# Attention output reloaded in two transfers a unit, with added waits between transfers

## The chip, the cores and the metric

The kernel runs on one core of a Trainium2 chip. The metric is the device time of one launch in microseconds (us); the kernel before takes 477.96 us, the median of three runs. On one core, TensorE (PE in the profile) multiplies, VectorE (DVE), ScalarE (ACT) and GpSimd (POOL) do the elementwise work, and SyncE (SP) issues the transfers, which the core's 16 DMA engines carry out.

## The reference

The input x has 2048 rows of 512 numbers. One layer normalization feeds two branches, whose product is added back to x.

```python
xn = layernorm(x)
q, k, v = split(xn @ wqkv)               # 32 heads of 16
# window of 8 positions, 2 apart: idx = pos - [0, 2, ..., 14], masked below 0
a = softmax(einsum(q, k[idx]) / 4)       # 8 logits for each row and head
s = einsum(a, v[idx]) @ wo               # attention, output projection 512 x 512
h = xn @ w1 + b1                         # 512 -> 1792
g = silu(relu(h) ** 2 @ w2 + b2)         # 1792 -> 512
out = x + s * g
```

## The kernel before

**Precision.** All large matmuls work on operands that are split into a high and a low part; a product takes three passes (high by high, high by low, low by high). So one block f of the down projection takes twelve matmuls with outputs of 128x512 (four row tiles by three passes), and the output projection of one row tile twelve as well (four parts of D by three passes). The splits cost ACT one instruction (the high part) and DVE or POOL one (the rest).

**First stage** (until about 267 us). The normalized rows are multiplied with wqkv. The results go to DRAM (`sq`, `sk`, `sv`) and come back unit by unit, a unit u being 256 rows (eight in all), in a layout that spreads eight groups of 64 columns (four heads) times 16 blocks of 16 rows over the 128 partitions. There DVE works the attention: products of k and q (`pr`), sums to logits (`L`), exponentials on ACT (`Lp`), products with v (`pv`), sums. The attention's output of a unit is written to DRAM, `so[g, row, 64]`. Beside it TensorE computes the up projection for the first and the second half of F; its outputs `u` stay on the chip for the rows of the chunks 0 and 1 and go to DRAM (`su`) for chunks 2 and 3, from where they come back as `ut`. DVE still works on the attention of the later units through most of the second stage.

**Second stage** (from about 267 us). A chunk c is 512 rows (four in all, each with two units, four row tiles t and four accumulators `pb`). For each block f of 128 of the 14 in F, `make_h` (line 1273) squares u on ACT and forms the rest on DVE or POOL, which gives the two parts of `h`; `down` adds twelve matmuls `pb<-w,h`. In a name such as h0_6 the first number is the chunk and the second the first block of the pair of tiles in it (h0_6 holds blocks 6 and 7). Chunk 0 also brings in w2 (`w2r` raw, one 128x512 transfer for each f, then split into `w`) and the output projection's weights: `load_wo` (line 1371) fetches each of `rwo0` and `rwo1` with two transfers of 256 KB, whose source is an access pattern of [4 groups of 128 rows, 32 rows, 512 columns], and `split_wo` (line 1377) makes `wot` of them. After the last block of a chunk comes the output projection of its first two row tiles (24 matmuls `pw<-wot,oT`), then the next chunk's blocks, and inside these the other two tiles.

**The attention's way back.** `load_o(u)` (line 1320) reads a unit of `so` into `oq`, of which there is one buffer; `trans_o(t)` (line 1329) transposes the half of it that belongs to row tile t in 32x32 blocks on DVE (`oTf`) and takes the high part on ACT (`oT`); `lowo` (line 1338) takes the rest; `out_product` (line 1341) multiplies with `wot`. In a tile's name the number is u for `oq`, and t for `oTf` and `oT`.

**What sets the order.** The program is built twice. In the first, the draft, every instruction is recorded with a price (`Book.add`, line 153), a list scheduler runs over them with these prices (a transfer: 600 ns to issue, then its bytes at 250 bytes a nanosecond on one wire shared by all), and the best of six rounds gives for every engine the order of its instructions, and for each "E" instruction whether it goes to DVE or POOL (`arrange`, line 377). The second program has the same instructions and a dependency between neighbours on each engine that keeps that order without a semaphore. Data and buffers bring their own waits. All transfers but those that load code are issued from SP in the order of the draft; eight semaphores serve them in turn, so that each transfer also waits for the one eight places ahead of it. Because everything passes through the recorder, every line of the profile reads L159, and tiles tell the instructions apart.

Of the kernel before, what the change touches and what calls it, by code (L numbers as in the profile page):

```python
# [11 lines left out]
F32 = mybir.dt.float32  # L12
FR = mybir.dt.float32r
AF = mybir.ActivationFunctionType
# [3 lines left out]
P = 128  # L18
S = 2048
# [11 lines left out]
UP = 256  # L31
NU = S // UP

GR = 8
CH = D // GR
# [43 lines left out]
def elements(ap):  # L79
    n = 1  # L80
    for d in ap.shape[1:]:
        n *= d
    return n


class Book:
# [66 lines left out]
    def add(self, key, name, f, a, k):  # L153
        n = len(self.ops)
        engine = key
        if key == "E":
            engine = self.plan[1][n] if self.plan else "V"
            f = getattr(f[engine], name)
        ins = f(*a, **k)  # L159
        out = k["out"] if "out" in k else a[0]  # L160
        outs = [out] + ([k["accum_out"]] if "accum_out" in k else [])
        ins_ = [*(a if "out" in k else a[1:]), *(x for i, x in k.items() if i not in ("out", "accum_out"))]
        ins_ = [x for x in ins_ if isinstance(x, bass.AP)]
        two = sum(x.space != bass.MemoryType.PSUM and elements(x) > 1 for x in ins_) > (name != "tensor_scalar")
        if key == "E":
            op = Op(n, "E", ins, {e: self.price(e, name, k, ins_, out) for e in "VG"}, True)
        elif name == "dma_start":
            moved = 4
            for d in out.shape:
                moved *= d  # L170
            op = Op(n, "S", ins, 600, moved=moved)
        else:
            op = Op(n, engine, ins, self.price(engine, name, k, ins_, out),
                    engine == "V" and two or engine == "G" and elements(out) > 1 and name != "memset")
        if self.first:
            if op.engine in self.heads:
                self.heads[op.engine].starts.append(op)
                op.waits += 1
            self.heads[op.engine] = op
        func = next((x for x in a if isinstance(x, mybir.ActivationFunctionType)), None)  # L180
        op.table = func if func in (AF.Exp, AF.Silu) else None
        op.stream = self.in_stream
        self.ops.append(op)
        if engine == "P":
            if "P" in self.last:
                self.edge(self.last["P"], op)
            self.last["P"] = op
        for x, writes in [(x, False) for x in ins_] + [(x, True) for x in outs]:
            r = self.region(x)
            if r is None:  # L190
                continue
            t, p0, p1, m = r
            writes = writes or t.space == "PSUM"
            if t not in op.tiles:
                op.tiles.append(t)
                if not t.users:
                    used = self.firsts.setdefault(t.slot, [])
                    if len(used) >= t.bufs:
                        t.behind = used[-1]
                    used.append(op)  # L200
                if t.behind not in (None, op):
                    t.behind.starts.append(op)
                    op.waits += 1
                t.users.append(op)
            kept = []
            for other, w, q0, q1, k_ in t.log:
                if (w or writes) and other is not op and p0 < q1 and q0 < p1 and m & k_:
                    self.edge(other, op)
                if not (writes and p0 <= q0 and q1 <= p1 and k_ & ~m == 0):
                    kept.append((other, w, q0, q1, k_))  # L210
            kept.append((op, writes, p0, p1, m))
            t.log = kept
        return ins
# [138 lines left out]
    def tails(self, order=None):  # L352
# [21 lines left out]
        top = max(tail)  # L374
        return [top - t for t in tail]

    def arrange(self):
        if self.plan is None:
            order, best = None, None
            for _ in range(ROUNDS):  # L380
                end, order = self.forward(self.tails(order))
                if best is None or end < best[0]:
                    best = end, [op.n for op in order], [op.given for op in self.ops]
            return best[1:]
        order = [self.ops[n] for n in self.plan[0]]
        for op in self.ops:
            op.given = self.plan[1][op.n]
        for e in "PVAGS":
            line = [op for op in order if op.given == e]
            for a, b in zip(line, line[1:]):  # L390
                self.tc.add_manual_dep(b.ins.ins, a.ins.ins.name, mybir.DependencyInfo(
                    mybir.DependencyClass.NoSync, mybir.DependencyReason.DATA), reason="order")


class Kept:
# [47 lines left out]
def trace(ctx: ExitStack, tc: tile.TileContext, plan, x, wqkv, wo, w1, b1, w2, b2, out):  # L443
# [4 lines left out]
    PE, V, A, G, E = (Recorded(book, n, e) for n, e in zip(  # L448
        "PVAGE", (nc.tensor, nc.vector, nc.scalar, nc.gpsimd, dict(V=nc.vector, G=nc.gpsimd))))
    dma = Recorded(book, "S", nc.sync).dma_start  # L450

    def pool(name, stack=ctx, after=(), **k):
        return Pool(book, stack.enter_context(tc.tile_pool(name=name, bufs=1, **k)), name, after)
# [125 lines left out]
    so = dram.tile([GR, S, CH], F32, name="so")  # L579
# [157 lines left out]
    mv, means, rs, shifts, xn, xb, pTs, seen, odd = ({} for _ in range(9))  # L737
# [291 lines left out]
    for a in range(2, NT, 2):  # L1029
        n, t = {2: 2, 4: 1}.get(a, 0), a + 2  # L1030
# [273 lines left out]
    p2 = pool("p2", ctx, (px, pstg, p2a, tpool))  # L1304
# [13 lines left out]
    oqs, oTs = {}, {}  # L1318

    def load_o(u):  # L1320

        if u in oqs:
            return
        oqs[u] = p2.tile([P, UP // 64, 2, 2, CH], F32, name=f"oq{u}", tag="oq")
        for g in range(GR):
            src = so[g, u * UP:(u + 1) * UP, :].rearrange("(b p e) c -> p b (e c)", p=32, e=2)
            dma(oqs[u][32 * (g // 2):32 * (g // 2) + 32, :, g % 2].rearrange("p b e c -> p b (e c)"), src)

    def trans_o(t):
        src = p2.tile([P, 512], F32, name=f"oTf{t}", tag="rwo", bufs=2)  # L1330
        src = src.rearrange("p (g n) -> p g n", g=4)
        V.transpose(out=src.rearrange("p (g h) (b n) -> p b g h n", h=2, n=32),
                    in_=oqs[t // 2][:, :, :, t % 2].rearrange("p b g (h c) -> p b g h c", c=32))
        oTs[t] = p2.tile([P, 2, 4, P], FR, name=f"oT{t}", tag="oT", bufs=3)
        A.activation(oTs[t][:, 0], src, AF.Copy)
        seen[t] = src

    def lowo(t):
        E.tensor_sub(oTs[t][:, 1], seen.pop(t), oTs[t][:, 0].bitcast(F32))

    def out_product(t, ps, cols=slice(0, D)):
        o = oTs[t]
# [50 lines left out]
    for c in range(NCH):  # L1393
        last = c == NCH - 1
        t0 = c * TPC
        for f in range(NF):
# [7 lines left out]
            if c:  # L1404
                if f < 2:
                    finish(t0 - 4 + f, E)
                if f == 2:
                    load_o(c * 2 - 1)
                    load_r(t0 - 2)
                    load_r(t0 - 1)  # L1410
                elif f == 4:
                    trans_o(t0 - 2)
                    trans_o(t0 - 1)
                elif f == 5:
                    lowo(t0 - 2)
                    lowo(t0 - 1)
                elif f == 6:
                    out_product(t0 - 2, psT(f"pw{t0 - 2}"))
                elif f == 7:
                    finish(t0 - 2, E)  # L1420
                    out_product(t0 - 1, psT(f"pw{t0 - 1}"))
                elif f == 8:
                    finish(t0 - 1, E)
            if f >= 7:
                load_o(c * 2)
            if f in (9, 10) and not last:
                load_r(t0 + f - 9)
            if f == 11:
                for i in range(2):
                    trans_o(t0 + i)  # L1430
            if f == 12:
                for i in range(2):
                    lowo(t0 + i)
                load_o(c * 2 + 1)
# [18 lines left out]
        else:  # L1453
# [15 lines left out]
            for j in range(2, TPC):  # L1469
                n = D // 2 if j == TPC - 1 else D  # L1470
# [28 lines left out]
```

## Time and profile before

| | |
|---|---|
| Runs, us | 479.42, 475.67, 477.96; median 477.96 |
| Profiled execution, us | 475.35, of which the span 473.6 |
| Mean granted TensorE clock | 0.996 |
| PE busy | 463.6 us, 98% of the span |
| DVE, ACT, POOL busy | 85%, 62%, 59% |
| Transfers of `oq` | 64 of 64 KB, eight a unit |
| Share of the chain that ended last | PE 89%, DMA 6%, all else 1% or less each |

The profile shows one execution. Its groups give, for each kind of instruction, the engine, the operation, output and inputs by tile names and the count, then busy time, the mean duration and the idle time just before with what ended it. In rows of a timeline stand the start in us, the duration of all instructions in the row, the engine and the group, the count behind an "x", and in brackets the idle time ahead of it and what it waited for. Rows of a stretch of time give its bounds and length, the busy time of PE, PEld (weight load), DVE, ACT and POOL with the number of instructions, then the granted TensorE clock, the busy share of the 16 DMA engines and what they moved in GB/s. Rows of the chain of waits give the start, the length and what ran or was waited for. DMA rows on SP (SPq) show how long issuing took, waits included.

### The profile page before, as it was taken

What the parts mean: (1) busy time and instruction counts of PE and PEld (TensorE: products, weight loads), DVE (VectorE), ACT (ScalarE), POOL (GpSimd) and SP (SyncE); (2) the same over time, 40 slices, a digit from 0 to 9 for tenths busy, and PEclk for the clock granted to TensorE, in tenths of its full rate; (3) what the DMA queues carried; (4) which work ended last, traced back from release to release, by engine and by line L of the source; (5) the groups of instructions that cost most, each with busy time, mean ns of one, the idle gap of its engine ahead of it and who ended that gap; (6) DMA issues with size and microseconds to landing.
All of it is one profiled execution on the core that took longest, in us unless ns stands there. A gap on an engine that the chain in (4) does not pass through costs nothing.

```text
span 473.6 us, 6218 instructions
## 1 busy us (share of the span) xinstructions
PE 463.6 (98%) x2037; PEld 380.6 (80%) x2037; DVE 403.9 (85%) x341; ACT 291.7 (62%) x567; POOL 280.5 (59%) x297
## 2 busy tenths in 40 slices
PE   8999999999999999999999997999999999999996
PEld 6788888888788888888888785788888888888886
DVE  4987977999999998999999984899999999992213
ACT  5756968866564558468584965795249535844311
POOL 2286324336997699956453567876674566376330
PEclk9999999999999999999999998999999999999999
DMA  8799899999689977641860558748894994443102
GB/s 276 210 219 280 287 220 285 253 230 252 184 226 275 261 239 201 227 105 47 209 155 2 156 144 205 193 124 251 174 255 115 259 238 142 146 144 91 45 19 72
DMA packets 77901, 87.78 MB, mean 185 GB/s; under 512 B 6956, under 2 KB 59436, under 8 KB 77868
## 3 DMA queue, kind: packets, MB, share of 16 engines
q1 hardware_dynamic: 77868, 87.38, 69.4%
q8 instruction: 16, 0.26, 0.2%
q14 instruction: 17, 0.14, 0.1%
HBM read 53.75 MB, written 30.47 MB: 178 GB/s over the span
## 4 chain that ended last, share of the span: by engine, by line
PE 89%; DMA 6%; POOL 1%; ACT 1%; DVE 1%; issue 1%; SPq 0%; POOLq 0%
PE pb L159 25%; PE uX L159 16%; PE pq L159 13%; PE pm L159 12%; PE pw L159 9%; PE uZ L159 8%; DMA w2r<-in_B_w 5%; PE uY L159 4%; DMA oq<-so 2%; PE warm L159 1%; SPq L159 0%; PE pxT L159 0%; POOL h L159 0%; DVE wq L159 0%; POOL w L159 0%
## 5 line engine op out<-in xcount | busy, mean ns | idle before, releaser
L159 PE MATMUL pb<-w,h 128*128 128x512 f32 x592 | 152.1, 394 | 3.6 <-POOL h L159 3.5
L159 PEld LDWEIGHTS pb<-w,h 128*128 128x128 f32 x592 | 111.6, 190 | 29.7 <-POOL h L159 5.8
L159 DVE TENSOR_TENSOR pr<-k,qp 128x2048 f32<-128x2048 f32 x32 | 72.8, 2276 | 7.3 <-ACT qp L159 5.6
L159 DVE TENSOR_REDUCE v<-pv 128x256 f32<-128x2048 f32 x32 | 73.0, 2281 | 0.7
L159 DVE TENSOR_TENSOR pv<-v,Lp 128x2048 f32<-128x2048 f32 x32 | 72.8, 2276 | 0.6
L159 DVE TENSOR_REDUCE L<-pr 128x128 f32<-128x2048 f32 x32 | 72.7, 2273 | 0.5
L159 POOL TENSOR_TENSOR h<-ut,h 128x512 fp32r<-128x512 f32 x26 | 33.3, 1295 | 34.6 <-ACT ut L159 33.3
L159 POOL TENSOR_TENSOR h<-u,h 128x512 fp32r<-128x512 f32 (+1 forms) x32 | 33.0, 1050 | 24.1 <-ACT u L159 16.8
L159 PE MATMUL pw<-wot,oT 128*128 128x512 f32 (+1 forms) x204 | 45.5, 376 | 0.0
L159 PEld LDWEIGHTS pw<-wot,oT 128*128 128x128 f32 x204 | 36.8, 188 | 7.1
L159 DVE TENSOR_TENSOR z<-z,pw 128x512 f32<-128x512 f32 (+1 forms) x17 | 11.0, 650 | 26.2 <-ACT z L159 14.4
L159 ACT ACTIVATE ut<-ut 128x512 f32<-128x512 f32 x42 | 24.8, 624 | 12.1 <-DMA ut<-su 12.0
L159 PE MATMUL pq<-wq,XA 128*128 128x512 f32 x122 | 31.5, 391 | 0.3 <-DVE wq L159 0.3
L159 ACT ACTIVATE u<-uX,b1t 128x512 f32<-128x512 f32 x28 | 19.2, 687 | 18.2 <-PE uX L159 14.6
L159 ACT ACTIVATE h<-ut 128x512 fp32r<-128x512 f32 x28 | 16.4, 625 | 22.3 <-PE pb L159 10.5
L159 POOL TENSOR_TENSOR u<-u,more 128x512 f32<-128x512 f32 x14 | 18.2, 1297 | 17.4 <-ACT more L159 16.7
L159 POOL TENSOR_TENSOR oT<-oTf,oT 128x512 fp32r<-128x512 f32 x16 | 20.7, 1295 | 11.3 <-ACT oT L159 11.3
L159 PEld LDWEIGHTS pq<-wq,XA 128*128 128x128 f32 x122 | 22.7, 188 | 5.4 <-DVE wq L159 0.7
L159 ACT ACTIVATE stg<-pm 128x512 f32<-128x512 f32 x30 | 18.0, 599 | 14.3 <-PE pm L159 12.0
L159 ACT ACTIVATE u<-u 128x512 f32<-128x512 f32 (+1 forms) x54 | 26.4, 528 | 0.2
L159 ACT ACTIVATE stg<-pq 128x512 f32<-128x512 f32 x24 | 14.3, 598 | 13.4 <-PE pq L159 10.8
L159 ACT ACTIVATE h<-u 128x512 fp32r<-128x512 f32 (+1 forms) x36 | 17.4, 528 | 5.9 <-PE pb L159 5.8
(166 smaller groups left out, 990.4 us busy)
## 6 DMA issues: line engine op xcount, KB each, us to landing
k<-sk SPq DMA_DIRECT2D x8, 960.0 KB
v<-sv SPq DMA_DIRECT2D x8, 960.0 KB, 7.1
su<-u SPq DMA_DIRECT2D x28, 256.0 KB, 2.5
ut<-su SPq DMA_DIRECT2D x28, 256.0 KB, 4.5
x<-in_A_x SPq DMA_DIRECT2D x16, 256.0 KB, 4.9
sk<-stg SPq DMA_DIRECT2D x8, 512.0 KB, 3.3
sq<-stg SPq DMA_DIRECT2D x8, 512.0 KB, 5.0
sv<-stg SPq DMA_DIRECT2D x8, 512.0 KB, 6.0
```

Of the source, the lines that this page charges most:

```text
L159: ins = f(*a, **k)
```

## The change

There are three edits. `load_o` fetches a unit with two transfers of 256 KB in place of eight of 64 KB: each fills all 128 partitions with 2 KB, read from four groups (outermost, 2·S·64 elements apart), 32 runs in each and 512 contiguous numbers a run. A partition then holds eight neighbouring rows of a group where it held rows 64 apart two by two; so the transposed rows stand in another order, and `trans_o` and `lowo` write `oT` through `positions`, with neighbouring elements four apart. And `landed` adds waits: for each transfer past the program's first part it looks up in the draft schedule which earlier transfer is the last one that has ended when this one starts, and makes it wait for that one, where that is later than what earlier transfers have waited for already.

```diff
--- before.py
+++ after.py
@@ -172,6 +172,7 @@
         else:
             op = Op(n, engine, ins, self.price(engine, name, k, ins_, out),
                     engine == "V" and two or engine == "G" and elements(out) > 1 and name != "memset")
+        op.early = self.first
         if self.first:
             if op.engine in self.heads:
                 self.heads[op.engine].starts.append(op)
@@ -374,13 +375,23 @@
         top = max(tail)
         return [top - t for t in tail]
 
+    def landed(self, order):
+
+        out, line, last = [], [op for op in order if op.moved], -1
+        for i, op in enumerate(line):
+            done = max((j for j in range(i) if line[j].end <= op.start), default=-1)
+            if done > last and not op.early:
+                out.append((op.n, line[done].n))
+                last = done
+        return out
+
     def arrange(self):
         if self.plan is None:
             order, best = None, None
             for _ in range(ROUNDS):
                 end, order = self.forward(self.tails(order))
                 if best is None or end < best[0]:
-                    best = end, [op.n for op in order], [op.given for op in self.ops]
+                    best = end, [op.n for op in order], [op.given for op in self.ops], self.landed(order)
             return best[1:]
         order = [self.ops[n] for n in self.plan[0]]
         for op in self.ops:
@@ -390,6 +401,9 @@
             for a, b in zip(line, line[1:]):
                 self.tc.add_manual_dep(b.ins.ins, a.ins.ins.name, mybir.DependencyInfo(
                     mybir.DependencyClass.NoSync, mybir.DependencyReason.DATA), reason="order")
+        for n, m in self.plan[2]:
+            self.tc.add_manual_dep(self.ops[n].ins.ins, self.ops[m].ins.ins.name, mybir.DependencyInfo(
+                mybir.DependencyClass.Sync, mybir.DependencyReason.DATA), reason="landed")
 
 
 class Kept:
@@ -1321,22 +1335,26 @@
 
         if u in oqs:
             return
-        oqs[u] = p2.tile([P, UP // 64, 2, 2, CH], F32, name=f"oq{u}", tag="oq")
-        for g in range(GR):
-            src = so[g, u * UP:(u + 1) * UP, :].rearrange("(b p e) c -> p b (e c)", p=32, e=2)
-            dma(oqs[u][32 * (g // 2):32 * (g // 2) + 32, :, g % 2].rearrange("p b e c -> p b (e c)"), src)
+        oqs[u] = p2.tile([P, 2, UP // 64, 2, CH], F32, name=f"oq{u}", tag="oq")
+        run = UP // 32 * CH
+        for g in range(2):
+            row = so[g, u * UP:u * UP + 1, :]
+            src = bass.AP(tensor=row.tensor, offset=row.offset, ap=[[2 * S * CH, GR // 2], [run, 32], [1, run]])
+            dma(oqs[u][:, g].rearrange("p b e c -> p (b e c)"), src)
 
     def trans_o(t):
         src = p2.tile([P, 512], F32, name=f"oTf{t}", tag="rwo", bufs=2)
-        src = src.rearrange("p (g n) -> p g n", g=4)
-        V.transpose(out=src.rearrange("p (g h) (b n) -> p b g h n", h=2, n=32),
-                    in_=oqs[t // 2][:, :, :, t % 2].rearrange("p b g (h c) -> p b g h c", c=32))
+        V.transpose(out=src.rearrange("p (g h b n) -> p b g h n", g=2, h=2, n=32),
+                    in_=oqs[t // 2][:, :, :, t % 2].rearrange("p g b (h c) -> p b g h c", c=32))
         oTs[t] = p2.tile([P, 2, 4, P], FR, name=f"oT{t}", tag="oT", bufs=3)
-        A.activation(oTs[t][:, 0], src, AF.Copy)
-        seen[t] = src
+        seen[t] = src.rearrange("p (g b n) -> p g b n", g=4, n=32)
+        A.activation(positions(t, 0), seen[t], AF.Copy)
+
+    def positions(t, a):
+        return oTs[t][:, a].rearrange("p g (n b) -> p g b n", b=4)
 
     def lowo(t):
-        E.tensor_sub(oTs[t][:, 1], seen.pop(t), oTs[t][:, 0].bitcast(F32))
+        E.tensor_sub(positions(t, 1), seen.pop(t), positions(t, 0).bitcast(F32))
 
     def out_product(t, ps, cols=slice(0, D)):
         o = oTs[t]
```

The transfers that SP issues fall from 312 to 264. The order of the instructions changes from about 268 us on. Three places show it. In the rows, the number behind an underscore only tells tiles of one name apart.

First the transfers on SP at the beginning of the second stage. Before:

```order
L159 DMA w2r8_2819<-in_B_w2 128x512
L159 DMA rwo0_2816<-in_A_wo 128x1x512 x2
L159 DMA oq0_2939<-so_155 32x4x128 x8
L159 DMA rwo1_2841<-in_A_wo 128x1x512 x2
L159 DMA w2r9_2844<-in_B_w2 128x512
L159 DMA w2r10_2864<-in_B_w2 128x512
L159 DMA v4_1539<-sv_154 128x1x1920
L159 DMA w2r11_2885<-in_B_w2 128x512
```

Now:

```order
L159 DMA w2r8_2819<-in_B_w2 128x512
L159 DMA rwo0_2816<-in_A_wo 128x1x512 x2
L159 DMA oq0_2939<-so_155 128x1x512 x2
L159 DMA rwo1_2841<-in_A_wo 128x1x512 x2
L159 DMA v4_1539<-sv_154 128x1x1920
L159 DMA w2r9_2844<-in_B_w2 128x512
L159 DMA w2r10_2864<-in_B_w2 128x512
L159 DMA w2r11_2885<-in_B_w2 128x512
```

The eight transfers of oq0 are two, of the shape that `rwo0` and `rwo1` have, and v4 (960 KB) has moved ahead of w2r9 and w2r10. Of the added waits, rwo1's second transfer waits for rwo0's first, v4 for rwo0's second, and w2r9 for rwo1's second. Some ten transfers later, the two of oq1 stand between ut2_0 and ut2_1, where the eight stood behind ut2_2.

Then ACT in the same stretch. Here `wot<-rwo1` is the split of the output projection's weights, h0_6 the squares of blocks 6 and 7 of chunk 0, qp5_2 a copy of q for the attention. Before:

```order
L159 ACTIVATE wot_2750<-rwo0_2816 128x512 x2
L159 ACTIVATE qp5_2_1553<-q5_1520 128x512
L159 ACTIVATE u06_2607<-u06_2607 128x2x256
L159 ACTIVATE wot_2750<-rwo1_2841 128x512
L159 ACTIVATE h0_6_2869<-u03_2454 128x512 x2
L159 ACTIVATE u03_2454<-u03_2454 128x2x256 x2
L159 ACTIVATE w28_2821<-w2r9_2844 128x512
L159 ACTIVATE w210_2866<-w2r10_2864 128x512
L159 ACTIVATE wot_2750<-rwo1_2841 128x512
```

Now:

```order
L159 ACTIVATE wot_2750<-rwo0_2816 128x512 x2
L159 ACTIVATE wot_2750<-rwo1_2841 128x512 x2
L159 ACTIVATE qp5_2_1553<-q5_1520 128x512
L159 ACTIVATE h0_6_2869<-u03_2454 128x512 x2
L159 ACTIVATE u03_2454<-u03_2454 128x2x256 x2
L159 ACTIVATE u06_2607<-u06_2607 128x2x256
L159 ACTIVATE w28_2821<-w2r9_2844 128x512
L159 ACTIVATE w210_2866<-w2r10_2864 128x512
L159 ACTIVATE h0_8_2915<-u04_2589 128x512 x2
```

Both copies of rwo1 stand ahead of qp5_2 and h0_6 now, where one of them stood behind qp5_2 and the other behind h0_6 and w210.

Last ACT in chunk 1, where TensorE works on its blocks 0 to 4; ut2_3 and the like are rectified there as they come back for chunk 2. Before:

```order
L159 ACTIVATE oT2_3215<-oTf2_3213 128x512
L159 ACTIVATE oT3_3219<-oTf3_3217 128x512
L159 ACTIVATE ut2_3_3394<-ut2_3_3394 128x512
L159 ACT_TABLE_LOAD
L159 ACTIVATE Lp5_1586<-L5_1543 128x512
L159 ACTIVATE ut2_5_3429<-ut2_5_3429 128x512
L159 ACTIVATE oT4_3388<-oTf4_3386 128x512
L159 ACTIVATE h1_4_3181<-u02_2445 128x512 x2
```

Now:

```order
L159 ACTIVATE oT2_3203<-oTf2_3201 128x4x4x32
L159 ACTIVATE oT3_3207<-oTf3_3205 128x4x4x32
L159 ACTIVATE ut2_3_3376<-ut2_3_3376 128x512
L159 ACT_TABLE_LOAD
L159 ACTIVATE Lp5_1586<-L5_1543 128x512
L159 ACTIVATE ut2_5_3405<-ut2_5_3405 128x512
L159 ACTIVATE ut2_7_3501<-ut2_7_3501 128x512
L159 ACTIVATE ut2_9_3541<-ut2_9_3541 128x512
L159 ACTIVATE h1_4_3169<-u02_2445 128x512 x2
```

The squares of blocks 4 and 5 (h1_4) follow ut2_7 and ut2_9 now, of which both stood behind them, and oT4 has gone behind them.

## The prediction

> **What bounds the kernel now.** I read the page first (span, busy times, shares of the chain), then busy times by stretch, then TensorE's timeline where a stretch loses time, then the chain of waits and the other engines' timelines there. The profiled execution took 475.35 us, its span is 473.6; the median of the runs is 477.96, and the mean of all four executions 477.1. Less than 1% either way, some 4.8 us, can't be told from no change here.
>
> ```profile
> span 473.6 us, 6218 instructions
> PE 463.6 (98%) x2037; PEld 380.6 (80%) x2037; DVE 403.9 (85%) x341; ACT 291.7 (62%) x567; POOL 280.5 (59%) x297
> PE 89%; DMA 6%; POOL 1%; ACT 1%; DVE 1%; issue 1%; SPq 0%; POOLq 0%
> ...
> 133.50:266.65 133.15, 133.15 (x589) 110.24 (x588) 130.36 (x80) 88.28 (x167) 94.69 (x106) 1.00 0.63 176
> 266.65:311.87 45.22, 41.62 (x170) 32.04 (x168) 34.68 (x22) 31.90 (x66) 32.12 (x28) 0.96 0.67 172
> 311.87:464.35 152.48, 152.48 (x674) 126.29 (x673) 121.71 (x86) 79.94 (x146) 85.45 (x70) 1.00 0.58 156
> ...
> 312.03 5.44 PE pw L159 x24
> ```
>
> TensorE is the bound: it has no idle time at all from 133.5 to 266.65 us and from 311.87 to 464.35 us. Only the stretch between, which is chunk 0, loses time. Its 14 blocks of 12 matmuls, at 5.44 / 24 = 0.227 us each by the last row, are 38.1 us of work in 45.2 us: 7.1 us are lost. That is the most that the change can win, 1.5%.
>
> ```profile
> 283.65 1.01 PE L159 MATMUL pb<-w,h 128*128 128x512 f32 x3
> 286.37 7.36 PE L159 MATMUL pb<-w,h 128*128 128x512 f32 x24 [1.71 <-POOL h L159]
> 295.02 2.33 PE L159 MATMUL pb<-w,h 128*128 128x512 f32 x9 [1.29 <-POOL h L159]
> ...
> PE pb L159 <- POOL h L159: 3.5, 4, 1.7
> ...
> 287.00:289.00 2.00, 2.00 (x7) 1.51 (x6) 0.00 (x0) 0.00 (x0) 0.56 (x1) 0.51 1.05 234
> ```
>
> Of the 7.1 us, 3.5 are waits for `h`, the longest ahead of block 6 at 286.37 us. The clock granted behind that pause is 0.51, and the 24 matmuls take 7.36 us where they would take 5.44: 1.9 more. The rest is slow first matmuls beside the pauses.
>
> Why was `h` late? ACT makes its high part, and ACT stood still:
>
> ```profile
> 275.97 1.14 ACT L159 ACTIVATE wot<-rwo 128x512 fp32r<-128x512 f32 x2
> 277.01 0.58 ACT L159 ACTIVATE qp<-q 128x512 f32<-128x512 f32 x1
> 282.73 0.63 ACT L159 ACTIVATE wot<-rwo 128x512 fp32r<-128x512 f32 x1 [4.57 <-DMA rwo<-in_A_wo]
> 283.26 1.14 ACT L159 ACTIVATE h<-u 128x512 fp32r<-128x512 f32 x2
> ...
> 268.14 8.07 DMA oq<-so
> 277.48 11.73 DMA w2r<-in_B_w
> ...
> 276.24 1.13 SPq L159 DMA_DIRECT2D rwo<-in_A_wo  x2
> ```
>
> It waited 4.57 us for the first half of rwo1, and the squares of blocks 6 and 7 stood behind that wait. The chain says the same in transfers: oq0's first, issued at 268.14, landed 8.07 us later at 276.2, then rwo1's two went out, and w2r9, issued at 277.48, landed at 289.2 behind them.
>
> **What the new transfers cost.** No transfer of oq of the new form is in the trace, but `rwo0` has the same one: 256 KB to all partitions, with four groups as the outermost part of the source. After its issue a stretch shows it nearly alone:
>
> ```profile
> 268.50:270.00 1.50, 1.50 (x8) 1.18 (x7) 1.50 (x2) 1.50 (x6) 0.20 (x1) 1.00 0.28 97
> 273.00:274.00 1.00, 1.00 (x6) 0.84 (x5) 1.00 (x1) 1.00 (x3) 1.00 (x3) 1.00 0.27 99
> 283.00:287.00 4.00, 2.29 (x10) 1.38 (x9) 3.85 (x2) 2.44 (x5) 1.95 (x2) 1.00 1.04 188
> ```
>
> The 16 DMA engines are busy for a share of 0.28 (4.4 of 16) at 97 GB/s, while a mixed load reaches 1.04 and 188 GB/s, or 234 by the row of 287 above. At 97 GB/s, 262 KB take 2.70 us; the two for a unit take 5.4 us. I take this value. The lower bound is the rate of all engines, 1.14 us each at 230 GB/s.
>
> [...]
>
> **Chunk 0, step by step.** T is the time at which rwo1's second half lands. At 276.2 the two halves of rwo0 are through (ACT splits them at 275.97 without a wait). oq0's first transfer, though only 64 KB and with a share for every engine, landed no sooner, so an engine works in the order of issue. I take it that two transfers of one form use the same engines; then oq0's two and rwo1's two stand in one line of four times 2.70 us: 276.2 + 10.8 = 287.0. v4 (960 KB), now right behind them, moves beside them. Before, rwo1's second half, which had v4 and three w2r beside it, landed between 282.7 and 289.2, so up to 6.5 us for 2.7 us of work. I add 1.5 us for v4: T = 288.5, with 287.0 as the end without contention.
>
> ACT now splits both halves of rwo1 ahead of qp5_2 and h0_6, so it stands still until T, where before it went on at 282.7 with the first half. Block 6 then follows by T + 0.6 (split) + 0.5 (qp5_2) + 3.1 (from h's start at 283.26 to TensorE's at 286.37) = 292.7, against 286.4: **+6.3**. The pause grows from 1.7 to 8 us, so the half clock lasts somewhat longer: I take 2.5 us for its 1.9, **+0.6**. The later stall of 1.29 us and one of 0.29 are covered then: **−1.6**. The end of chunk 0 moves by **+5.3** us, from 311.9 to 317.2.
>
> [...]
>
> w2r9 waits for rwo1's second half too, so the queue (w2r9 to w2r11, q6, xr, w2r12, w2r13) starts at 288.5; block 9 is needed only at 292.7 + 3 x 2.72 = 300.9, and I cost that at nothing. If v4 or w2r came 5 us later, block 9 would be late by some 2 us.
>
> **Chunk 1.** qp5_2 also starts DVE's next attention step:
>
> ```profile
> L159 DVE TENSOR_TENSOR pr<-k,qp 128x2048 f32<-128x2048 f32 x32 | 72.8, 2276 | 7.3 <-ACT qp L159 5.6
> L159 DVE STREAM_TRANSPOSE oTf<-oq x16: 669/700/711, 295.4 to 438.6; 128x512 f32<-128x512 f32 x16
> L159 DVE TENSOR_TENSOR w212r<-w2r,w x1: 1106/1106/1106, 303.1 to 303.1; 128x512 fp32r<-128x512 f32 x1
> ...
> 306.15 0.71 ACT L159 ACTIVATE h<-u 128x256 fp32r<-128x256 f32 x2
> 314.02 0.73 ACT L159 ACTIVATE h<-u 128x256 fp32r<-128x256 f32 x2
> 318.16 1.28 ACT L159 ACT_TABLE_LOAD   x1
> ...
> ut<-su SPq DMA_DIRECT2D x28, 256.0 KB, 4.5
> ```
>
> In the new order DVE does five attention steps of 2.28 us, three parts of `h` of 1.1 us (as w212r) and two transposes of 0.70 before oq0's second transpose is over: 16.1 us. From T + 1.1 and half a microsecond of hand-overs that is 306.4, where oq's single buffer is free. oq1's two transfers (5.4 us) then go ahead of ut2_1 (4.5 us from issue to landing): 316.3. ACT rectifies ut2_1 ahead of h1_0, and from the start of h1_0 to the end of h1_1 it took 7.9 us (306.15 to 314.02): 324.4, and the low part 0.7 more, 325.1. TensorE wants block 1 at 317.2 + 5.44 + 2.72 = 325.4: just in time, 0. Then ACT does h1_2 (2.5 us), two oT (1.0), ut2_3 (0.6), a table load (1.3), Lp (0.5), ut2_5, 7 and 9 (1.6) and h1_4 (1.6), and POOL its low part (1.3): 324.4 + 10.4 = 334.8, while TensorE wants block 4 at 325.4 + 3 x 2.72 = 333.6: **+1.3**, rounded with the hand-over. Afterwards the slack is larger.
>
> **What costs nothing.** SP's issue time shrinks (eight oq took 7.94 us of issue, mostly waits), but TensorE never waited for SP. The waits added earlier, from SP's fifteenth transfer on, hold back transfers whose predecessors are still on the wire; DVE is busy for 130.4 of 133.2 us there, and TensorE has no gap. I take 0, between 0 and +2. The strided `oT` is taken at 0: POOL's first low part runs at 301.16 us, 10.7 ahead of its matmul at 311.87.
>
> ```profile
> 301.16 1.29 POOL L159 TENSOR_TENSOR oT<-oTf,oT 128x512 fp32r<-128x512 f32 x1
> 311.87 5.60 PE L159 MATMUL pw<-wot,oT 128*128 128x512 f32 x24
> ...
> oq<-so SPq DMA_DIRECT2D x64, 64.0 KB, 3.5
> ```
>
> Were it twice as slow (16 x 1.3 = 21 us more on POOL, 59% busy), it would still be in time in most chunks.
>
> Sum: 5.3 + 1.3 = **+6.6**, that is 482.0 on the profiled execution and 483.7 on the mean of the four: I say 484.
>
> **Rivals.** *The forecast*, +3.5 to +10: for it speak the row of 97 GB/s and ACT's order. 54%.
>
> *Worse*, +10 to +16: oq0's and rwo1's transfers each take up to 6.5 us, as rwo1's second half may have, and ACT is held again in chunk 1 by a late ut2_9. Against it: v4 is only 4 us of traffic at 230 GB/s. 8%, 489 to 493.
>
> *All engines, others, or absorbed*, within 1%: if the new oq goes over other engines than rwo, T = 276.2 + 5.4, with v4 beside it 283.1; if it spreads over all, T = 276.2 + 2 x 1.14 + 2 x 2.70 = 283.9, with contention up to 286.2, and block 6 starts at 288.1 to 290.4; less the 1.6 given back, 0 to +2.4. Or T is 287.0, and nothing is lost in chunk 1. For it: the old oq of 64 KB took 3.5 us with all engines; against it: the form is rwo's. 31%, 475 to 480.
>
> *Faster*: the whole loss of chunk 0 goes, which needs block 6 by its due time of 284.7, so T by 280.5. Then up to 7.1 us are won, 468 to 471 on the profile, about 471 as measured. For that the rwo transfers would have to run at the rate of all engines too. 7%. [...]
>
> So faster 7%, the same 31%, slower 62%. The range reaches from 476, for most of the absorbed cases, to 491.
>
> **What would show it.** oq's two transfers with a DMA share near 0.28, landing 5 us or more behind rwo0; ACT standing still for 10 us before `wot<-rwo`; a stall of about 8 us ahead of block 6 in place of 1.71, with the clock at half behind it; 1 to 2 us of idle TensorE before block 4 of chunk 1; no gap from 340 us on. I am wrong if oq lands at the rate of all engines, if ACT's copy waits no longer than before, or if TensorE has gaps ahead of 266 us, where the added waits would be to blame.

## The result, and the profile after

The change made the kernel slower: 493.71 us median (492.91 to 494.6, four runs) against 476.89 (four runs of before). The ratio is 1.0346, with a 95% interval from 1.0295 to 1.0397. The direction was forecast; the amount was not, as 493.71 lies above the range's end of 491. The profiled execution took 493.88 us, 18.5 more than that of before.

From the profile of the changed kernel, its span, busy times and chain by engine:

```profile
span 492.1 us, 6152 instructions
PE 468.2 (95%) x2037; PEld 382.1 (78%) x2037; DVE 407.8 (83%) x345; ACT 301.2 (61%) x569; POOL 281.4 (57%) x293
PE 62%; DMA 17%; DVE 9%; ACT 4%; issue 4%; POOL 2%; SPq 1%; DVEq 0%; POOLq 0%; ACTq 0%
```

TensorE's share of the chain fell from 89% to 62%, and DMA's rose from 6% to 17%. The stretches are chunk 0 first, then two in which transfers of the slow form stand alone. The columns are as before.

```profile
133.50:266.65 133.15, 133.15 (x589) 110.23 (x589) 130.36 (x80) 88.08 (x166) 94.88 (x107) 1.00 0.64 176
266.65:311.87 45.22, 37.32 (x149) 29.13 (x148) 30.89 (x20) 26.84 (x54) 28.91 (x24) 0.89 0.59 162
272.00:276.00 4.00, 4.00 (x19) 3.28 (x18) 3.28 (x3) 4.00 (x9) 3.67 (x5) 1.00 0.26 100
284.00:288.00 4.00, 0.23 (x2) 0.00 (x0) 0.00 (x0) 0.63 (x1) 0.00 (x0) 0.94 0.27 100
```

Up to 266.65 us TensorE is as busy as before: the added waits there cost nothing. In 272 to 276 us and in 284 to 288 the DMA engines move 100 GB/s at a share of 0.26 and 0.27, the same as rwo alone before (0.28 at 97 GB/s). In 272 to 276 the transfers of rwo0, oq0 and rwo1 had been issued (SP's rows below), and the share did not rise, so they sat on the same engines; the experiments below bear this out. From 284 to 288 what was left moved at that rate, and DVE and POOL did nothing and TensorE and ACT next to nothing.

TensorE's timeline, and the start of the output projection's matmuls (pw) as marks between the chunks:

```profile
290.60 1.22 PE L159 MATMUL pb<-w,h 128*128 128x512 f32 x2 [6.37 <-ACT h L159]
293.04 10.44 PE L159 MATMUL pb<-w,h 128*128 128x512 f32 x35 [1.22 <-POOL h L159]
...
316.69 5.60 PE L159 MATMUL pw<-wot,oT 128*128 128x512 f32 x24
335.79 0.73 PE L159 MATMUL pb<-w,h 128*128 128x512 f32 x2 [2.11 <-ACT h L159]
338.24 4.37 PE L159 MATMUL pb<-w,h 128*128 128x512 f32 x11 [1.72 <-POOL h L159]
344.97 2.88 PE L159 MATMUL pw<-wot,oT 128*128 128x512 f32 x12
...
391.17 2.77 PE L159 MATMUL pb<-w,h 128*128 128x512 f32 x11 [1.71 <-POOL h L159]
414.08 6.19 PE L159 MATMUL pb<-w,h 128*128 128x512 f32 x26 [0.88 <-POOL h L159]
421.70 1.43 PE L159 MATMUL pb<-w,h 128*128 128x512 f32 x5 [1.20 <-DVE h L159]
444.95 2.79 PE L159 MATMUL pb<-w,h 128*128 128x512 f32 x11 [1.72 <-POOL h L159]
482.71 5.75 PE L159 MATMUL pw<-wot,oT 128*128 128x512 f32 x36
```

The marks of before for the same matmuls were 311.87 (shown with the prediction) and these:

```profile
333.63 2.88 PE L159 MATMUL pw<-wot,oT 128*128 128x512 f32 x12
464.19 5.75 PE L159 MATMUL pw<-wot,oT 128*128 128x512 f32 x36
```

So 4.8 us are lost up to the end of chunk 0, 344.97 − 333.63 − 4.8 = 6.5 more in the first half of chunk 1, and 18.5 − 11.3 = 7.2 later, spread over pauses in chunks 2 and 3. The profiled execution of before is a fast one, 475.35 against a median of 476.89, so these parts are in sum 1.7 us more than the medians differ by. SP's issues, the chain's transfers, ACT's waits and DVE's:

```profile
267.02 1.23 SPq L159 DMA_DIRECT2D rwo<-in_A_wo  x2
268.30 1.08 SPq L159 DMA_DIRECT2D oq<-so  x2
269.48 4.95 SPq L159 DMA_DIRECT2D rwo<-in_A_wo  x2
...
267.02 5.82 DMA rwo<-in_A_wo
272.86 16.00 DMA rwo<-in_A_wo
307.87 8.34 DMA ut<-su
329.99 4.51 DMA ut<-su
...
286.21 0.63 ACT L159 ACTIVATE wot<-rwo 128x512 fp32r<-128x512 f32 x1 [8.91 <-DMA rwo<-in_A_wo]
288.88 0.63 ACT L159 ACTIVATE wot<-rwo 128x512 fp32r<-128x512 f32 x1 [2.04 <-DMA rwo<-in_A_wo]
334.59 0.63 ACT L159 ACTIVATE ut<-ut 128x512 f32<-128x512 f32 x1 [1.91 <-DMA ut<-su]
...
DVE oTf L159 <- DMA oq<-so: 21.4, 5, 8.8
```

The chain names rwo1's second half, which was issued at 272.86 and landed 16 us later. ACT waited 8.91 and 2.04 us for the two halves. In chunk 1 it waited for ut2_9, and DVE stood five times at a transpose until oq had landed, 21.4 us in all. In the kernel before that was

```profile
DVE oTf L159 <- DMA oq<-so: 3.6, 2, 2.8
```

(us in total, times, the longest).

### The profile page after: what moved, and what is told of

It is laid out like the page before. It is cut to its first block, busy times and chain, and to the rows that moved or that the text cites. A ratio compares the mean times of both kernels' runs of the same rounds, so it can differ in the third digit from the quotient of the medians.

```text
span 492.1 us, 6152 instructions
## 1 busy us (share of the span) xinstructions
PE 468.2 (95%) x2037; PEld 382.1 (78%) x2037; DVE 407.8 (83%) x345; ACT 301.2 (61%) x569; POOL 281.4 (57%) x293
## 4 chain that ended last, share of the span: by engine, by line
PE 62%; DMA 17%; DVE 9%; ACT 4%; issue 4%; POOL 2%; SPq 1%; DVEq 0%; POOLq 0%; ACTq 0%
PE uX L159 15%; PE pq L159 13%; PE pm L159 11%; PE uZ L159 8%; PE pb L159 6%; DMA rwo<-in_A_wo 4%; PE uY L159 4%; PE pw L159 3%; DMA oq<-so 3%; DMA ut<-su 3%; DMA q<-sq 2%; DVE pv L159 2%; DVE v L159 2%; DMA k<-sk 2%; DMA v<-sv 2%
## 5 line engine op out<-in xcount | busy, mean ns | idle before, releaser
L159 PE MATMUL pb<-w,h 128*128 128x512 f32 x592 | 156.6, 400 | 17.5 <-ACT h L159 8.5
L159 PEld LDWEIGHTS pb<-w,h 128*128 128x128 f32 x592 | 113.0, 193 | 46.6 <-POOL h L159 10.5
L159 POOL TENSOR_TENSOR h<-u,h 128x256 fp32r<-128x256 f32 (+1 forms) x29 | 29.2, 1021 | 38.6 <-issue 19.5
L159 POOL TENSOR_TENSOR h<-ut,h 128x512 fp32r<-128x512 f32 x24 | 31.1, 1308 | 34.3 <-ACT ut L159 23.8
L159 ACT ACTIVATE ut<-ut 128x512 f32<-128x512 f32 x42 | 25.0, 625 | 32.5 <-DMA ut<-su 32.5
L159 POOL TENSOR_TENSOR oT<-oTf,oT 128x512 fp32r<-128x512 f32 x16 | 25.7, 1611 | 13.7 <-ACT oT L159 13.7
L159 DVE STREAM_TRANSPOSE oTf<-oq 128x512 f32<-128x512 f32 x16 | 11.1, 700 | 25.0 <-DMA oq<-so 21.4
```

## The experiments

Three theories were set against each other: that few DMA engines carry the new transfers, that the added waits hold the queue back, and that the new order of the instructions costs time.

**two_no_waits**

```diff
-        for n, m in self.plan[2]:
+        for n, m in ():
```

> Two transfers a unit as in the change, the added waits left out; every engine has the change's order. Theory 1 (few engines): oq's transfers are slow because four of the 16 DMA engines carry them, so nearly all of the 16.8 us stay: 488 to 495, DVE still waits some 20 us for oq. Theory 2 (waits): the added waits hold the queue back, so 476 to 482. Theory 3 (order): the change's order of the instructions is what costs, so 490 to 495, and relaid is as slow.

Measured: 496.10 us (495.32 to 496.98), ratio 1.0396 [1.0356, 1.0436]. DVE waited 21.3 us for oq. This is above the ranges of theories 1 and 3 and far above theory 2's: the loss stays without the waits. It is 18.6 us over the kernel before timed beside it (477.46), against 16.8 with the waits. By stretch, the two profiles differ both ways. The same marks as above stand at 317.92, 343.17 and 485.16 us without the waits, so chunk 0 ends 1.2 us later, the first half of chunk 1 takes 25.25 us in place of 28.28, and the rest 141.99 in place of 137.74. In these two executions the waits cost 3.0 us in chunk 1 and save 4.2 later.

**eight_with_waits**: the kernel before with `landed` and its dependencies added, `load_o` left as it was.

```diff
+        for n, m in self.plan[2]:
+            self.tc.add_manual_dep(self.ops[n].ins.ins, self.ops[m].ins.ins.name, ...)
```

> The kernel before with the added waits alone; its transfers and its order are those of before. Theory 1: 475 to 481. Theory 2: 485 or more. Theory 3: 475 to 481.

Measured: 477.42 us against 477.46, ratio 1.0 [0.9984, 1.0017]. By themselves the waits cost nothing.

**relaid**

```diff
-    so = dram.tile([GR, S, CH], F32, name="so")
+    so = dram.tile([NU, GR, UP, CH], F32, name="so")
...
-            src = bass.AP(..., ap=[[2 * S * CH, GR // 2], [run, 32], [1, run]])
+            src = bass.AP(..., ap=[[run, P], [1, run]])
...
-            row = wo[64 * i + 32 * g:64 * i + 32 * g + 1, :]
-            dma(rwo[i][:, g], bass.AP(..., ap=[[P * D, 4], [D, 32], [1, D]]))
+            row = wo[256 * i + 32 * g:256 * i + 32 * g + 1, :]
+            dma(rwo[i][:, g], bass.AP(..., ap=[[64 * D, 4], [D, 32], [1, D]]))
```

> The change's order, waits and two transfers of 256 KB a unit, but so is laid out in DRAM by units, so that a transfer's source is 128 runs of 512 numbers and has no outer dimension of four (the rows of wo go with it). Theory 1: oq's transfers land in about 2.5 us when alone, DMA share of all engines, and the time is 474 to 482. Theory 2: 485 or more, since the waits are all there. Theory 3: 490 to 495, since the order is the change's.

Measured: 476.84 us (475.4 to 478.33), ratio 0.9986 [0.9968, 1.0005]. Order, waits, count and bytes are those of the change; what differs is where so and the rows of wo lie in DRAM and, with it, the shape of oq's source, and all of the loss is gone. A transfer of oq landed 2.9 us after its issue at the least and 6.5 in the median, with others beside it. DVE's waits for oq in this profile:

```profile
DVE oTf L159 <- DMA oq<-so: 1.5, 1, 1.5
```

They fell from 21.4 us to 1.5. As causes of the whole loss, the waits and the order are out. What is left of the change, two transfers in place of eight, is worth nothing measurable.

**relaid_no_waits**, the edit of two_no_waits on relaid.

> relaid without the added waits. Theory 1: 472 to 480, within 3 us of relaid. Theory 2: 474 to 480, 8 us or more below relaid. Theory 3: 490 to 495.

Measured: 477.38 us, ratio 0.9996 [0.998, 1.0012], half a microsecond from relaid.

**halves_2 and quarters_32** tell whether the outermost dimension of the source decides. The first fetches a unit with four transfers to 64 partitions each, the second with four to 32 partitions.

```diff
# halves_2
+            for h in range(2):
+                row = so[4 * h + g, u * UP:u * UP + 1, :]
+                src = bass.AP(..., ap=[[2 * S * CH, 2], [run, 32], [1, run]])
+                dma(oqs[u][64 * h:64 * h + 64, g]..., src)
# quarters_32
+        for g in range(GR // 2):
+            row = so[2 * g, u * UP:u * UP + 1, :]
+            src = bass.AP(..., ap=[[run, 32], [S * CH, 2], [1, run]])
+            dma(oqs[u][32 * g:32 * g + 32]..., src)
```

> The change with so as before, but four transfers of 128 KB a unit, each to 64 partitions, so that the outermost dimension of the source has size 2. Its order is that of quarters_32. If the outermost size sets the number of engines and these are the same for all such transfers: two engines carry all of oq, a DMA share of 0.13 when alone, 2.6 us a transfer and 10.5 a unit, and the time goes well beyond the change's, 505 to 530. If small runs or the place in DRAM make oq slow: as the change, 488 to 498, and quarters_32 too.

> As halves_2 with the same order, count and bytes, but each transfer goes to 32 partitions, so that the outermost size is 32. If the outermost size sets the engines: all engines, 472 to 480. If not: 488 to 498.

Measured: halves_2 530.03 us (528.9 to 531.21), ratio 1.1097 [1.1068, 1.1126]; quarters_32 478.28 us, ratio 1.0005 [0.999, 1.0019]. halves_2 comes out at the upper end of its first range, quarters_32 inside its own. Count, bytes, order and the place in DRAM are the same, and 52 us lie between them. In the profile of halves_2, a stretch behind the issue of rwo0 and the next, in which oq0's are left:

```profile
272.00:274.00 2.00, 2.00 (x11) 1.63 (x10) 1.71 (x1) 2.00 (x5) 2.00 (x3) 1.00 0.26 97
274.00:276.00 2.00, 2.00 (x11) 1.65 (x10) 1.58 (x1) 2.00 (x5) 2.00 (x3) 1.00 0.13 50
```

With an outermost size of four the share is 0.26 at 97 GB/s; with two it is 0.13 at 50. The packets in the traces show the engines at work. From 272 to 276 us in the changed kernel four packets of 2 KB were under way for 3.25 of the 4 us and never fewer, though five transfers of this form were waiting or under way; in halves_2 it was two for 1.70 of the 2 us from 274 on; in relaid, while oq1 came in from 304.4 to 305.0, sixteen or more for most of the time. A packet took 84 or 85 ns in each, so one such engine moves some 24 GB/s; 0.26 of 16 engines is 4.2 and 0.13 is 2.1, and the others stay idle. So an outermost size of two came with a share of 0.13 and one of four with 0.26, and with 32 and 128 nothing was lost (quarters_32 at 478.28 us, relaid at 476.84). Joining small transfers won nothing: eight of 64 KB and two of 256 KB over all engines take 477.46 and 476.84 us.

**slow_0, slow_12 and slow_3up** are relaid with a gap between the groups of some units only, so that the source of these alone has four groups outermost. `slow` below is (0,), (1, 2) or (3, 4, 5, 6, 7).

```diff
+    pitch = [(UP + (u in slow)) * CH for u in range(NU)]
...
-            src = bass.AP(..., ap=[[run, P], [1, run]])
+            runs = [[pitch[u], GR // 2], [run, 32]] if u in slow else [[run, P]]
+            src = bass.AP(..., ap=runs + [[1, run]])
```

> relaid (fast transfers, the change's order and waits), with the two transfers of oq0 alone in the slow form (source of four groups, by a gap between the groups). Theory A (each unit costs where it stands): chunk 0 ends some 3 us later than in relaid and nothing follows, 478.5 to 481.5. Theory B (cascade: oq0's delay moves DVE's attention and through it all later units): 486 or more.

> relaid with oq1 and oq2 alone in the slow form. Theory A: chunk 0 as in relaid, a pause ahead of block 4 of chunk 1 through the late ut2_9, 479 to 484. Theory B: 477 to 479, since it all begins with oq0.

> relaid with oq3 to oq7 alone in the slow form. Theory A: chunks 0 and 1 as in relaid, pauses of 2 to 3 us each around the units of chunks 2 and 3, 481 to 486; the three parts (slow_0, slow_12, slow_3up) add up to some 17 us above relaid. Theory B: 477 to 479.

Measured: 480.05 us, ratio 1.0048 [1.0024, 1.0073]; 484.17 us, ratio 1.0127 [1.0097, 1.0156]; 485.76 us, ratio 1.0162 [1.0135, 1.0188]. Above relaid's 476.84 these are 3.2, 7.3 and 8.9 us, 19.4 in sum, against 16.9 for the change; slow_12 lies just above its range, the other two inside. The sum is 2.5 us too high, so the parts don't add up exactly. Their profiles place each loss. Where relaid has the marks at 313.41, 335.17 and 465.73 us, slow_0 has 316.63, 338.39 and 468.95: 3.2 us in chunk 0 and none after. slow_12 has 312.67, 343.23 and 473.79: 8.8 in the first half of chunk 1 and none after. slow_3up has 312.66, 334.42 and 475.10: 10.1 after the second mark and none before. Each unit costs where it stands; it is no cascade from oq0.

**relaid_rwo and before_rwo_quarters** give the weights of the output projection the better shape, on top of relaid and alone. In the kernel before:

```diff
-        for g in range(2):
-            row = wo[64 * i + 32 * g:64 * i + 32 * g + 1, :]
-            dma(rwo[i][:, g], bass.AP(..., ap=[[P * D, 4], [D, 32], [1, D]]))
+        for g in range(4):
+            row = wo[P * g + 64 * i:P * g + 64 * i + 1, :]
+            dma(rwo[i][32 * g:32 * g + 32], bass.AP(..., ap=[[D, 32], [32 * D, 2], [1, D]]))
```

> relaid with the weights of the output projection in four transfers of 32 partitions for each of rwo0 and rwo1 (128 KB each, slowest dimension 32) in place of two with four groups outermost. If few engines are also what delays rwo1, and that delay is the loss in chunk 0: rwo1 lands before 280 us, most of the 7 us of chunk 0 come back, 469 to 473. If the transfers are late for another reason, or another wait takes over: 474 to 478.

> The kernel before with rwo0 and rwo1 in four transfers of 32 partitions each, nothing else. If rwo's few engines are the loss of chunk 0 in the kernel before too: 468 to 473, as relaid_rwo, and the change's own parts are worth nothing beside it. If the two transfers of oq are needed for the gain: 474 to 478.

Measured: 469.45 us, ratio 0.9818 [0.9794, 0.9842], and 469.16 us, ratio 0.9821 [0.98, 0.9842]. Both are about 1.8% faster than the kernel before and 5% faster than the changed one, and they are equal: the change's own parts add nothing. Busy times and chunk 0 in the profile of relaid_rwo:

```profile
PE 460.7 (99%) x2037; PEld 379.8 (81%) x2037; DVE 411.1 (88%) x346; ACT 301.4 (64%) x569; POOL 280.5 (60%) x292
266.65:311.87 45.22, 44.90 (x197) 36.47 (x196) 43.04 (x28) 38.32 (x80) 37.67 (x33) 1.00 0.77 204
```

TensorE is busy for 44.90 of the 45.22 us in which it had 41.62 before, and the clock no longer falls (1.00, where it was 0.96). In relaid_rwo both copies of rwo1 still stand ahead of the squares of blocks 6 and 7 on ACT; rwo's transfers land 3.2 to 4.5 us after their issue, and ACT's waits for them, 4.71 and 3.17 us in relaid, are gone. So there the few engines of rwo were the loss of chunk 0. In before_rwo_quarters the draft also gave another order, with both copies of rwo1 behind these squares. How much of its gain is the shape of the transfers and how much the order was not separated. The prediction had priced this at "up to 7.1 us", under the condition that the rwo transfers run at the rate of all engines; 8 to 9 were measured.

**relaid_rwo_no_waits**

> relaid_rwo without the added waits. With all transfers fast there is little for the waits to hold back: within 2 us of relaid_rwo, 468 to 472. If the waits keep ACT's and SP's transfers in a good order: 473 or more.

Measured: 469.45 us, ratio 0.9826 [0.9805, 0.9847], the same as relaid_rwo.

**slow_12_no_waits and slow_3up_no_waits**, the edit of two_no_waits on the two parts.

> slow_12 without the added waits. Theory A1 (the wait passes the delay on): in slow_12 ut2_5 and all behind it go out only when oq2's second transfer has landed, so ut2_9 is late for ACT; without the wait they go out early, ut2_9 lands in time, the pause ahead of block 4 goes, 477 to 480. Theory A2 (the engines pass it on): a transfer over all 16 engines queues behind oq2 on its few engines anyway, and lands as late: 482 to 486.

> slow_3up without the added waits. A1: below 482, with shorter waits of DVE for oq. A2 (DVE stands at its transposes until oq has landed, and the waits matter little): 484 to 488, with DVE's waits for oq of some 20 us in sum as before.

Measured: 481.31 us (480.7 to 481.37), ratio 1.0087 [1.0057, 1.0117], and 490.08 us (486.09 to 491.28), ratio 1.026 [1.0209, 1.0312]. The first lies between the ranges of its two theories, the second above both. In chunk 1 the waits carry 2.9 of the 7.3 us by the medians. By the profiles the first half of chunk 1 takes 30.56 us in slow_12, 25.14 without the waits and 21.76 in relaid, so that 5.4 of 8.8 us go with the waits; the end of chunk 0, 1.8 us later without them, hides a part of that in the total. Both theories had a part. ACT's wait for ut2_9 in slow_12, then in slow_12_no_waits:

```profile
332.20 0.63 ACT L159 ACTIVATE ut<-ut 128x512 f32<-128x512 f32 x1 [2.29 <-DMA ut<-su]
```

```profile
330.86 0.63 ACT L159 ACTIVATE ut<-ut 128x512 f32<-128x512 f32 x1 [0.32 <-DMA ut<-su]
```

In the later chunks the waits save time, about 4 us of medians, though the runs without them spread over 5. DVE's waits for oq there, with and without the added waits:

```profile
DVE oTf L159 <- DMA oq<-so: 22.8, 5, 9.1
```

```profile
DVE oTf L159 <- DMA oq<-so: 24.0, 5, 7.8
```

It stands at the transposes for the same time either way, so here the wait goes with the transfers' form, not with the added waits. A part of the 4 us is the clock: in chunks 2 and 3 slow_3up has one stretch at half clock (0.58 from 382 to 386 us) and slow_3up_no_waits two (0.58 from 409 to 412, 0.57 from 440 to 444). Why the clock fell once more there was not settled, nor where the rest comes from.

## Why the prediction was right or wrong

**Bound and price: right.** 2.70 us a transfer at 97 GB/s was taken from rwo's row; that the new oq would run on rwo's engines was an estimate of mine, which no trace of before showed. The share of 0.26 at 100 GB/s confirms both. So do the semaphores in the trace: the two transfers each of rwo0, oq0 and rwo1 landed at 272.84, 275.52, 278.18, 283.65, 286.19 and 288.86 us, one behind the other and 2.5 to 2.7 us apart, but for 5.5 us in which v4, issued at 275.53, moved beside them. Even the trace of before shows the line: twelve of the sixteen updates for oq0's first transfer had come by 271.2 us, the last four came from 275.5 on, when rwo0 was through. T was forecast at 288.5, and 288.86 is partly luck: the line began 0.7 us earlier than taken, and v4 cost 2.8 us where 1.5 were taken.

**Chunk 0: right.** Block 6 was forecast at 292.7; its first two matmuls ran at 290.60 and the rest from 293.04, the second waiting for POOL. The end of chunk 0 moved by 4.8 us where 5.3 were forecast. Of these, slow_0 gives 3.2 to the new oq0 alone. The other 1.6 are there without a slow oq too: the output projection starts at 313.65 us in eight_with_waits, which has the order of before, and in relaid at 313.41:

```profile
313.41 5.60 PE L159 MATMUL pw<-wot,oT 128*128 128x512 f32 x24
```

The clock's term was right as well: 35 matmuls behind the pause took 10.44 us in place of 35 × 0.227 = 7.9, so 2.5 as taken. The longer pause cost more than the short one of before: the clock was granted at half for 10.2 us here, from 287.5 us on, and for 3.4 us there, from 287.0 on.

**Chunk 1: the step that failed.** Its forecast was +1.3, and 6.5 were measured. The first half of the working held: oq1's transfers were forecast to go out at 306.4 and ut2_1 to land at 316.3, and they were issued at 306.62 and the chain has ut2_1 through at 307.87 + 8.34 = 316.2. (The sum on the way has 0.4 us too much: 288.5 + 1.1 + 0.5 + 16.1 is 306.2, and 316.3 + 7.9 is 324.2.) But for ut2_5, ut2_7 and ut2_9 the sum counted only the 1.6 us that ACT works on them, as if they had landed. Ahead of them stand oq2's two transfers, which I did not price. SP in this stretch:

```profile
306.62 1.14 SPq L159 DMA_DIRECT2D oq<-so  x2
307.87 1.28 SPq L159 DMA_DIRECT2D ut<-su  x2
317.10 1.14 SPq L159 DMA_DIRECT2D oq<-so  x2
318.75 12.46 SPq L159 DMA_DIRECT2D ut<-su  x8
```

oq2 went out at 317.10, held until ut2_2 had landed. The eight ut behind it took 12.46 us to issue, and for 6.2 of these SP waited for oq2, as ut2_5 waits for its second transfer. In relaid the same eight began at 310.81 and took 10.12. The last that h1_4 needs, issued at 329.99 by the chain, landed at 334.5. Two more things that the sum had at nothing stand in the 6.5. Without the added waits this stretch lost 3.5 (25.25 us in two_no_waits, where the kernel before takes 21.76), so 3.0 came through them; and 1.5 of these are the clock, which fell to half behind the pause, so that the 11 matmuls from 338.24 took 4.37 us, against 2.83 for the same 11 without the waits:

```profile
340.00:342.00 2.00, 2.00 (x6) 1.54 (x6) 2.00 (x3) 0.91 (x2) 2.00 (x3) 0.50 1.04 242
```

I had named this very wait in the worse rival, with +10 to +16 and 8%, and put it down there to v4's contention in chunk 0, not to oq2's own place in the queue.

**Chunks 2 and 3: the second step that failed.** "Afterwards the slack is larger" gave 0 without a sum, and 7.2 us were lost. The five late units cost 8.9 us in slow_3up. TensorE paused for 0.9 to 1.7 us at four places for parts of `h`, 5.5 us in all, and slower matmuls beside the pauses, at full clock (1.00 from 342.1 us to 492.3), make up the rest. Two ways lead there, and the sentence on the slack has neither. One is that DVE works in order: each unit's transpose waits for oq, up to 8.8 us, and the attention steps and parts of `h` queued behind it are late. The chain shows it for the pause that ends at 421.70:

```profile
393.05 9.19 DMA oq<-so
402.36 0.13 DVE oTf L159
420.96 0.69 DVE h L159
```

The other is that `ut` lands late, as in chunk 1. ACT's waits for it are 32.5 us in all in the changed kernel, where they were 12.0, and with the late units alone slow they go from the first row (relaid) to the second (slow_3up):

```profile
ACT ut L159 <- DMA ut<-su: 1.9, 1, 1.9
ACT ut L159 <- DMA ut<-su: 26.5, 7, 7.0
```

How much of the 7.2 us goes by each way stays open. Luck has a part in it: a pause of 1.71 us ahead of block 6 halved the clock in the kernel before, and one of 1.71 us at 391.17 in the changed kernel did not (1.00 from 391 to 393 us).

**No cost: mostly right.** The early waits cost nothing. The strided `oT` was put at 0 and costs work, but none that the total shows: in the profile of the changed kernel,

```profile
L159 ACT ACTIVATE oT<-oTf x16: 1108/1134/1188, 296.4 to 474.1; 128x512 fp32r<-128x512 f32 x16
L159 POOL TENSOR_TENSOR oT<-oTf,oT x16: 1553/1564/2026, 299.6 to 475.9; 128x512 fp32r<-128x512 f32 x16
```

and of that before,

```profile
L159 ACT ACTIVATE oT<-oTf x16: 613/630/642, 299.7 to 453.5; 128x512 fp32r<-128x512 f32 x16
```

the median of ACT's is 1.13 us, from 0.63; POOL's is 1.56, from 1.29. relaid has the same strided writes and no loss. In chunk 1 two of ACT's stand ahead of h1_4 and take 2.10 us where the sum had 1.0, but ACT waits for ut2_9 after them.

**Rivals.** That the new oq spreads over all engines was the case for "within 1%"; relaid made it true and measured 476.84, inside it. That rwo at the rate of all engines makes the kernel 471 was the case for faster; relaid_rwo measured 469.45.

## What to carry to other kernels

Read the busy share of the DMA engines in a stretch where one transfer is alone. A share near 0.26 or 0.13 at an even 100 or 50 GB/s meant here that four or two engines carried it, and the outermost dimension of its access pattern is the first thing to change; here that, with the order that the draft made of it, was worth 1.8% on a kernel whose TensorE was 98% busy. When a transfer gets slower, price every place where it stands, with what is queued behind it on SP and on the engine that waits for it; a comparison of landing and use misses the engines that work in order, as DVE did here (21.4 us at transposes that waited for oq).

## What the runs showed that I had not expected

Cutting rwo into twice as many transfers of half the size took the kernel from 478.16 to 469.16 us, its order changed with it, while joining oq's from eight to two changed nothing once all engines carried them. And added waits between transfers, which cost nothing with fast transfers (477.42 against 477.46 us), lost 2.9 us in one place (slow_12) and saved about 4 in another (slow_3up) with slow ones; in the change itself its profiles have 3.0 lost and 4.2 saved at the same two places.
